# Gates of a mixture layer turned in 32x32 blocks by VectorE instead of 128x128 by TensorE, with one gate factor moved to ScalarE and GpSimd

## The chip, the cores and the metric

One core of a Trainium2 chip runs the whole program. Its five engines are named as in the profile: PE (TensorE, matrix products), DVE (VectorE), ACT (ScalarE), POOL (GpSimd) and SP (which only issues transfers here). The metric is the device time of one execution in microseconds (us), the median of several runs; lower is better.

## The reference, cut to what matters

Attention with mixed heads gives x, of 1792 tokens by 768. Two layers follow; the change lies in the first and in the part of the second that uses its gates. N is 1792, D 768, F 2048, and there are 32 slots (8 experts by 4).

```python
h = x @ w_in                          # 1792 x 2048
g = h - np.tanh(h)
x = g @ w_out                         # 1792 x 768
logits = x @ phi                      # 1792 x 32
d = softmax(logits, axis=0)           # over tokens
slot_input = d.T @ x                  # 32 x 768
slot_out[e] = relu(slot_input[e] @ w1[e]) @ w2[e]    # 8 experts
c = softmax(logits, axis=1)           # over slots
out = c @ slot_out
```

The product `g @ w_out` is never formed. The kernel folds w_out and phi into `wphi` (2048 x 32), so that logits = g @ wphi; it keeps `SA`, the sum over tokens of d times g (32 x 2048), and multiplies that with w_out at the end.

## The kernel before, in words

**Stages.** Up to about 496 us the attention runs; the first two products of the next stage already stand between its last matmuls. `moe_and_slots` then works through the tokens in four passes of 512, 512, 512 and 256 tokens (`PASS`). A pass has 16 steps, one for each 128 columns of w_in; step t = 16 b + f is step f of pass b. After the last step come the logits of the last pass, the slot sums, the products with w_out, and the eight experts (`hidden`, `finish`, `slot_out`, from 840 us), whose weights stream in through a ring of buffers of 1536 KB (`free`, `give`, `load_expert`).

**A step.** `step(t)` issues everything by hand: each engine runs its instructions in the order in which the code gives them. `product(t)` is 18 matmuls (6 blocks of 128 inputs, three terms each: high and low parts of weight and input) into one of three PSUM banks. Between the six blocks it calls the hooks that `on(c, ...)` has put there. While PE forms product t, the other engines work on the gate of step t-1: `gate_act` (ACT: square of h into `sq`, a second square with a shift into `qd`, tanh into `g`, a mask `mk`), `gate_poly` and `gate_first` (DVE: two products that finish the polynomial in `qd`, then h - tanh), and `gate_last` (DVE: the third product, then the polynomial is copied where h is small). `sq` lies in the PSUM banks q0 and q1.

**The turn.** The slot sums contract over tokens, but a gate has the 128 columns on partitions and tokens along the row. So `turn_g(t-2)` lets PE transpose the gate in 128x128 blocks into PSUM (four matmuls in the first three passes, two in the last; tile `gt`), and ACT copies the result into one of five `quad` buffers (L826, L829). In the next pass `slot_turn` does the same for the exponentials of the 32 slots (`etp`, L946), and `slot_sum`, in two halves in steps 4 and 5, multiplies: 4 token blocks by 4 groups of columns, each a matmul with 128 rows, 32 columns of weights and 512 columns of data into one of the four 32-partition strips of one bank (L958). One DVE instruction adds the bank to `SA` (L966). After the last step the same is done for the last pass, and `dt` (L1152) turns `SA` with four matmuls.

**Weights.** In the first pass ACT and POOL split each weight tile into high and low parts (`split_w`, L707 and L708) and store both for the next passes (`wis`); the first pass also turns w_out (`wt`). In the last pass the tile is loaded anew and split in halves: `split_half(t+1, 0)` on DVE and `split_half(t+1, 1)` on ACT, with the low parts from POOL (L717).

Of the kernel before, what the change touches and what calls it, by code (L numbers as in the profile page):

```python
# [566 lines left out]
def moe_and_slots(tc, ident, xd, wi, wo, wo4, wis, consts, w1, w2, out, box):  # L567
# [5 lines left out]
    tshift, tlimit, phi, sel, sela, seld = consts  # L573
# [17 lines left out]
    XW = KD * TM  # L591
    RU = 2 * DM
# [29 lines left out]
    quad, quad_a, quad_b = [xep.tile([128, FB * NRM], FP32, tag=f"quad{i}", name="quad") for i in range(3)]  # L622
# [120 lines left out]
    hps, quads, tok = {}, {}, {}  # L743
# [26 lines left out]
    def gate_act(t, beside=None):  # L770
        hp = hps[t]
        if t > 1:
            mem["sq"] = {t: bank(f"q{t % 2}", [128, PASS[t // NF]], "sq")}
        sq, qd, mk, g = temps_of(t)
        nc.scalar.activation(out=sq, in_=hp, func=ACTF.Square)  # L775
        nc.scalar.activation(out=qd, in_=sq, func=ACTF.Square, bias=tshift)
        if t >= LAST:
            gate_poly(t)
# [39 lines left out]
    def turn_g(t):  # L818
        b, f = divmod(t, NF)
        n = blocks[b]  # L820
        if f % NG == 0:
            tok[b, f // NG] = place(b, f // NG)
        g = g_of(t)
# [3 lines left out]
        i = f % NG  # L827
        dst = tok[b, f // NG].rearrange("p (r f) -> p r f", r=n)[:, :, i * 128:(i + 1) * 128]
        nc.scalar.activation(out=dst, in_=x, func=ACTF.Copy)  # L829

    def place(b, k):
        if b == NPASS - 1:
            n = blocks[b] * FB
            return quads["C" if k < 2 else "D"][:, k % 2 * n:(k % 2 + 1) * n]
        return quads["AECDB"[(b * NQ + k) % 5]]
# [571 lines left out]
```

## Time and profile before

| | |
|---|---|
| median of 3 runs | 930.33 us (929.08 to 930.88) |
| the profiled execution | 929.89 us |
| its span, first to last instruction | 928.2 us |
| mean granted TensorE clock | 0.988 of full speed |
| busy, share of the span | PE 97%, PEld 71%, DVE 61%, ACT 62%, POOL 32% |

The profile is one execution. PE is TensorE's matmuls and PEld its weight loads, which run beside them. A matmul of plain 32-bit floats shows as two records, one of the fp32r kind as one, a transpose as one. A row with a tile name `a<-b` writes a and reads b. Idle time is put down to what ended it.

### The profile page before, as it was taken

The page shows a single profiled execution, that of the slowest core. Times are in us where ns is not written, and L with a number is a line of the kernel's source. Part 1 is how long each engine was busy: PE and PEld are TensorE (multiplying, and loading weights), DVE is VectorE, ACT ScalarE, POOL GpSimd, SP SyncE. Part 2 cuts the span into 40 slices and gives each one's busy share as a digit, 9 for nine tenths or more (in the row PEclk, how much of TensorE's full clock was granted, in tenths as well). Part 3 has the DMA queues.
Part 4 walks back from the last instruction along what each step waited for, and adds up shares of the span by engine and source line. Part 5 has one row for each costly group of instructions (what it writes and reads, how often), then busy time and mean ns, then how long its engine had stood idle before and what let it go on. Part 6 is the DMA issues. An engine that isn't in the chain of part 4 may idle for free.

```text
span 928.2 us, 19426 instructions
## 1 busy us (share of the span) xinstructions
PE 898.9 (97%) x6926; PEld 659.8 (71%) x6926; DVE 564.2 (61%) x1267; ACT 574.0 (62%) x1299; POOL 296.5 (32%) x499
## 2 busy tenths in 40 slices
PE   8999999999999999999999999999999999999995
PEld 6667777777777777777777777767776776874542
DVE  3576667767577676786555567567766776740104
ACT  4776767777677777777666576646664665730113
POOL 1464445644456444565432222000000014610000
PEclk9999999999999999999999999999999999998997
DMA  6988688976889567674467868769764445879997
GB/s 134 241 219 234 190 242 226 235 216 200 230 233 267 179 201 215 205 249 145 144 238 246 324 232 269 257 243 365 290 226 157 155 131 187 314 297 425 422 389 279
DMA packets 143988, 223.95 MB, mean 241 GB/s; under 512 B 60756, under 2 KB 125332, under 8 KB 140052
## 3 DMA queue, kind: packets, MB, share of 16 engines
q1 hardware_dynamic: 140544, 209.83, 70.3%
q10 hardware_dynamic: 3348, 12.87, 3.6%
q8 instruction: 56, 0.92, 0.4%
q14 instruction: 40, 0.33, 0.1%
HBM read 147.96 MB, written 36.18 MB: 198 GB/s over the span
## 4 chain that ended last, share of the span: by engine, by line
PE 90%; DMA 3%; ACT 3%; DVE 2%; issue 1%; POOL 0%; ACTq 0%; POOLq 0%; SPq 0%; DVEq 0%
PE hp L755 24%; PE pm L297 15%; PE tm L333 14%; PE vx L357 8%; PE sc L266 7%; PE h L1195 3%; DMA D<-S 3%; PE gt L826 3%; PE so L1234 2%; PE tz L1213 2%; PE lgp L876 2%; PE sp L958 1%; PE wt L845 1%; PE qx L245 1%; PE wp L857 1%
## 5 line engine op out<-in xcount | busy, mean ns | idle before, releaser
L333 PEld LDWEIGHTS tm<-wk,e 120*112 120x112 f32 (+1 forms) x1440 | 174.0, 177 | 70.7 <-issue 58.9
L299 DVE TENSOR_REDUCE mx<-pm 120x1 f32<-120x448 f32 x180 | 111.9, 622 | 125.2 <-PE pm L297 124.6
L336 ACT ACTIVATE aT<-tm 112x480 f32<-112x480 f32 x180 | 105.4, 586 | 120.5 <-PE tm L333 120.5
L297 PE MATMUL pm<-D,wpre 120*120 120x448 f32 x360 | 174.2, 566 | 3.8 <-DMA D<-S 2.2
L333 PE MATMUL tm<-wk,e 120*112 120x120 f32 (+1 forms) x1440 | 176.7, 266 | 1.0 <-POOL wk L323 1.0
L323 POOL TENSOR_SCALAR wk<-wpost,rv 120x120 f32<-120x120 f32 x180 | 125.0, 695 | 136.2 <-PE tm L333 115.2
L755 PE MATMUL hp<-xa,rg 128*128 128x512 f32 x576 | 152.5, 405 | 0.0
L755 PEld LDWEIGHTS hp<-xa,rg 128*128 128x128 f32 x576 | 102.4, 188 | 28.5 <-issue 10.7
L306 ACT ACTIVATE e<-pm,mx 120x448 f32<-120x448 f32 x180 | 113.5, 631 | 4.9 <-DVE rv L318 2.3
L717 POOL TENSOR_TENSOR rg<-rg 128x384 fp32r<-128x384 f32 x32 | 32.0, 1013 | 207.9 <-DVE rg L714 193.8
L274 ACT ACTIVATE S<-sc 120x448 f32<-120x448 f32 (+1 forms) x186 | 90.7, 543 | 5.3 <-PE sc L266 3.0
L357 PE MATMUL vx<-aT,vn 112*64 112x120 f32 (+1 forms) x1536 | 84.0, 262 | 0.0
L786 DVE SCALAR_TENSOR_TENSOR qd<-qd,sq 128x512 f32<-128x512 f32 (+1 forms) x62 | 38.3, 617 | 71.6 <-ACT mk L782 63.5
L357 PEld LDWEIGHTS vx<-aT,vn 112*64 112x64 f32 x1536 | 73.9, 137 | 6.2 <-issue 1.1
L775 ACT ACTIVATE sq<-hp 128x512 f32<-128x512 f32 (+1 forms) x62 | 32.9, 530 | 72.6 <-PE hp L755 72.6
L755 PE MATMUL hp<-xb,rg 128*128 128x512 f32 x288 | 74.7, 404 | 0.0
L312 POOL TENSOR_SCALAR rv<-ss 120x1 f32<-120x1 f32 x180 | 43.0, 239 | 96.8 <-ACT e L306 84.6
L297 PEld LDWEIGHTS pm<-D,wpre 120*120 120x120 f32 x360 | 51.4, 182 | 26.4 <-issue 11.4
L266 PE MATMUL sc<-khi,qT 64*120 64x448 f32 (+1 forms) x384 | 68.8, 387 | 0.8 <-DVE qT L249 0.8
L68 POOL TENSOR_TENSOR fa<-fa,f 128x384 f32<-128x384 f32 x64 | 65.3, 1020 | 5.3 <-issue 0.3
L755 PEld LDWEIGHTS hp<-xb,rg 128*128 128x128 f32 x288 | 52.0, 188 | 16.6 <-issue 6.3
L708 POOL TENSOR_TENSOR rg<-rg 128x768 fp32r<-128x768 f32 x13 | 24.0, 1844 | 67.9 <-PE gt L826 33.5
(173 smaller groups left out, 1356.9 us busy)
## 6 DMA issues: line engine op xcount, KB each, us to landing
ex<-in_moe_w_dram SPq DMA_DIRECT2D x25, 1536.0 KB
D<-S SPq DMA_DIRECT2D x172, 210.0 KB
rg<-wis SPq DMA_DIRECT2D x32, 768.0 KB
f<-in_moe_w_in_dram SPq DMA_DIRECT2D x32, 384.0 KB
f<-in_moe_w_out_dram SPq DMA_DIRECT2D x32, 384.0 KB
wis<-rg ACTq DMA_DIRECT2D x16, 768.0 KB
rg<-wi SPq DMA_DIRECT2D x26, 384.0 KB
wi<-fa SPq DMA_DIRECT2D x32, 192.0 KB
```

Source lines behind the costliest of these rows:

```text
L68: eng.tensor_tensor(out=out, in0=bits(a), in1=bits(p), op=ALU.add)
L266: nc.tensor.matmul(xs[e][0][:ni], lhsT=qT[n][s, l, p, :ni], rhs=kt[s], start=(i == 0), stop=(i == 2))
L274: nc.scalar.activation(out=dst, in_=xs[e][0][:ni], func=ACTF.Copy)
L297: nc.tensor.matmul(x[:r], lhsT=wpre[:r, :m, :], rhs=D_t.pop(s)[:r], start=True, stop=True)
L299: nc.vector.tensor_reduce(out=mx[:r], in_=x[:r], op=ALU.max, axis=AX.X, negate=True)
L306: nc.scalar.activation(out=e[:r], in_=pp_t.pop(s)[:r], func=ACTF.Exp, bias=mx_t.pop(s)[:r], accum_out=ss[:r])
L312: nc.gpsimd.tensor_scalar(out=rv[:r], in0=ss_t.pop(s)[:r], scalar1=EPS, scalar2=None, op0=ALU.add)
L323: nc.gpsimd.tensor_scalar(out=wk[:r], in0=wpost[:r], scalar1=ss_t.pop(s)[:r], scalar2=None, op0=ALU.mult)
L333: nc.tensor.matmul(x[:, c, :, :m], lhsT=e[:r, c * JP:(c + 1) * JP], rhs=wk[:r, :, :m], start=True, stop=True)
L336: nc.scalar.activation(out=attn_t[n][:, :, :, c0:c0 + m], in_=x[:, :, :, :m], func=ACTF.Copy)
L357: nc.tensor.matmul(x[64 * e:64 * e + 64, i, :ni], lhsT=nat_v[b, h // NP][:, h % NP, c, :], rhs=a[:, c, h, :ni], start=(c == 0), stop=(c == ...
L755: nc.tensor.matmul(hp, lhsT=r32(w[:, m, hl, cs]), rhs=r32(x_of(b, c, l)), start=(c == 0 and i == 0), stop=(c == KD - 1 and i == 2))
```

## The change

It turns the gates on DVE. `turn_g` becomes one or two DVE transposes that turn every 32x32 block of a gate in place of PE's 128x128 transposes and ACT's copy; the blocks go to `turned[0]` (`tq`) and `turned[1]` (`th`), 8 token blocks of 32 each. They hold one pass, so the turns of steps 0 to 2 of a pass wait until its step 4, behind the slot sum of the pass before (in the first pass those of steps 0 to 4 wait until step 6). `slot_turn` is one DVE transpose. `slot_sum` is a single piece at the end of step 3: 64 matmuls of 32 rows by 32 columns with 512 columns of data (32 in the last pass), in four banks (q0, q1, r0, r1) by four strips. `SA` grows to 128 x 2048 and takes four DVE updates; `dt` takes 16 matmuls.

The gate: `sq` moves to SBUF, ACT forms `sa` = sq - A, POOL multiplies it with sq, and DVE's two products of the polynomial become one (steps 2 to 47). In the last pass both split copies go to ACT, behind the two squares. Three `quad` buffers become one of twice the size; the last pass gives two buffers instead of three to the experts' ring. The scratch for dynamic transfers goes from 1024 to 256 bytes.

```diff
     def split_half(t, m):
             h, l = unit(t)[:, m, 0], unit(t)[:, m, 1]
-            if m == 0:
-                nc.vector.tensor_copy(out=r32(h), in_=l)
-            else:
-                nc.scalar.activation(out=r32(h), in_=l, func=ACTF.Copy)
+            nc.scalar.activation(out=r32(h), in_=l, func=ACTF.Copy)
             nc.gpsimd.tensor_tensor(out=r32(l), in0=l, in1=h, op=ALU.subtract)
...
     def gate_act(t, beside=None):
-            mem["sq"] = {t: bank(f"q{t % 2}", [128, PASS[t // NF]], "sq")}
+            mem["sq"] = {t: mem["sb"][:, :PASS[t // NF]]}
         nc.scalar.activation(out=sq, in_=hp, func=ACTF.Square)
+        if 1 < t < LAST:
+            sa = mem["sa"][:, :PASS[t // NF]]
+            nc.scalar.activation(out=sa, in_=sq, func=ACTF.Identity, bias=tminus)
+            nc.gpsimd.tensor_tensor(out=sa, in0=sa, in1=sq, op=ALU.mult)
         nc.scalar.activation(out=qd, in_=sq, func=ACTF.Square, bias=tshift)
...
     def gate_first(t):
-        if t < LAST:
-            gate_poly(t)
+        if 1 < t < LAST:
+            nc.vector.scalar_tensor_tensor(out=qd, in0=qd, scalar=TG_E, in1=sa, op0=ALU.add, op1=ALU.mult)
         nc.vector.tensor_tensor(out=g, in0=hp, in1=g, op=ALU.subtract)
...
     def turn_g(t):
         b, f = divmod(t, NF)
-        x = turn_bank([128, n, 128], "gt")
-        for r in range(n):
-            nc.tensor.transpose(out=x[:, r, :], in_=g[:, r * 128:(r + 1) * 128], identity=ident)
-        nc.scalar.activation(out=dst, in_=x, func=ACTF.Copy)
+        g = g_of(t).rearrange("p (b l) -> p b l", l=NSL)
+        for part in range(0, PASS[b] // NSL, NTB // 2):
+            nc.vector.transpose(out=turned[part * 2 // NTB][:, :, f, :], in_=g[:, part:part + NTB // 2, :])
...
-    def slot_sum(b, lo, hi):
+    def slot_sum(b):
+        n = PASS[b] // NSL
+        xs = [bank(tag, [128, NF, NSL], "sp") for tag in ("q0", "q1", "r0", "r1")]
+        for tb in range(n):
+            g = tb % NG
+            rows = turned[tb * 2 // NTB][:, tb % (NTB // 2)]
+            for i in range(NG):
+                p = slice(NSL * i, NSL * i + NSL)
                 nc.tensor.matmul(
-                    x[NSL * k:NSL * k + NSL, :], lhsT=es[:, r, :], rhs=tok[b, k][:, r * FB:(r + 1) * FB],
+                    xs[i][NSL * g:NSL * g + NSL], lhsT=es[p, tb * NSL:(tb + 1) * NSL], rhs=rows[p],
+                    start=(tb < NG), stop=(tb >= n - NG))
+        for i in range(NG):
+                nc.vector.scalar_tensor_tensor(out=s, in0=s, scalar=a, in1=xs[i], op0=ALU.mult, op1=ALU.add)
...
-    dt = bank("h2", [128, NG, 128], "dt")
-    for i in range(NG):
+    dt = bank("h2", [128, NF, NSL], "dt")
+    for i in range(NF):
         nc.tensor.matmul(dt[:, i, :], lhsT=mem["SA"][:, i * 128:(i + 1) * 128], rhs=sr, start=True, stop=True)
...
-    nc = _bacc.Bacc("TRN2", target_bir_lowering=False, num_devices=1, dynamic_dma_scratch_size=1024)
+    nc = _bacc.Bacc("TRN2", target_bir_lowering=False, num_devices=1, dynamic_dma_scratch_size=256)
```

**What moves on PE, second pass, steps 3 and 4.** Of the kernel before (`hp` is a step's product, `gt` a turn of a gate, `etp` that of the exponentials, `sp` the slot sum of the first pass):

```order
L826 MATMUL gt<-ident,g 128x128 x4
L755 MATMUL hp<-xb,rg 128x512 x6
L946 MATMUL etp<-ident,et 128x32 x4
L755 MATMUL hp<-xb,rg 128x512 x12
L826 MATMUL gt<-ident,g 128x128 x4
L755 MATMUL hp<-xb,rg 128x512 x3
L958 MATMUL sp<-quad,es 32x512 x2
L958 MATMUL sp<-tq,es 32x512 x2
```

and of the change, from the small products of step 2 on:

```order
L882 MATMUL ln<-seld,lp 128x32 x4
L754 MATMUL hp<-xb,rg 128x512 x27
L946 MATMUL sp<-tq,es 32x512 x32
L946 MATMUL sp<-th,es 32x512 x32
L754 MATMUL hp<-xb,rg 128x512 x36
L865 MATMUL lgp<-g,wphi 32x512 x4
```

The turns are gone, the slot sum stands in one piece behind step 3, and its matmuls are 64 where they were 16.

**What moves on DVE, one step late in the third pass (`xc` is the next pass's tokens being split).** Before:

```order
L786 SCALAR_TENSOR_TENSOR qd<-qd,sq 128x512
L787 SCALAR_TENSOR_TENSOR qd<-sq,qd 128x512
L794 TENSOR_TENSOR g<-hp,g 128x512
L799 SCALAR_TENSOR_TENSOR hp<-qd,hp 128x512
L800 COPY_PREDICATED g<-mk,hp 128x512
L741 TENSOR_TENSOR xc<-xc 128x256
```

and now (`L797` is the shortened polynomial, `STREAM_TRANSPOSE` the turn):

```order
L797 SCALAR_TENSOR_TENSOR qd<-qd,sa 128x512
L798 TENSOR_TENSOR g<-hp,g 128x512
L803 SCALAR_TENSOR_TENSOR hp<-qd,hp 128x512
L804 COPY_PREDICATED g<-mk,hp 128x512
L824 STREAM_TRANSPOSE tq<-g 128x8x32
L824 STREAM_TRANSPOSE th<-g 128x8x32
L740 TENSOR_TENSOR xc<-xc 128x256
```

One product of the polynomial goes, two turns of 256 columns each come.

**What moves on ACT, one step of the last pass.** Before:

```order
L775 ACTIVATE sq<-hp 128x256
L776 ACTIVATE qd<-sq,tshift 128x256
L716 ACTIVATE rg<-rg 128x384
L781 ACTIVATE g<-hp 128x256
L782 ACTIVATE mk<-sq,tlimit 128x256
L829 ACTIVATE tq<-gt 128x2x128
```

and now:

```order
L774 ACTIVATE sq<-hp 128x256
L779 ACTIVATE qd<-sq,tshift 128x256
L715 ACTIVATE rg<-rg 128x384 x2
L784 ACTIVATE g<-hp 128x256
L785 ACTIVATE mk<-sq,tlimit 128x256
```

The copy of a turned gate (`L829`) goes, and the first split copy, DVE's before, comes in behind the second square.

## Rows read from the trace of the kernel before

**Rows 1.** The page, parts 1 and 4: engines' busy time; the chain by engine

```profile
PE 898.9 (97%) x6926; PEld 659.8 (71%) x6926; DVE 564.2 (61%) x1267; ACT 574.0 (62%) x1299; POOL 296.5 (32%) x499
...
PE 90%; DMA 3%; ACT 3%; DVE 2%; issue 1%; POOL 0%; ACTq 0%; POOLq 0%; SPq 0%; DVEq 0%
```

**Rows 2.** Windows: stretch, length, busy us per engine (instructions), PE clock, DMA share, GB/s

```profile
501.00:585.50 84.50, 82.59 (x460) 61.02 (x459) 54.20 (x89) 57.14 (x101) 22.12 (x12) 1.00 0.79 274
...
760.00:818.00 58.00, 52.64 (x408) 43.63 (x408) 41.56 (x110) 38.91 (x102) 29.96 (x30) 0.97 0.65 225
...
840.00:905.00 65.00, 62.96 (x687) 30.76 (x686) 4.92 (x19) 7.03 (x14) 2.17 (x8) 0.92 1.02 411
```

**Rows 3.** Timeline of PE, two steps of the third pass: start us, length us

```profile
733.22 4.36 PE L755 MATMUL hp<-xa,rg 128*128 128x512 f32 x18
...
737.77 4.35 PE L755 MATMUL hp<-xa,rg 128*128 128x512 f32 x18
```

**Rows 4.** The chain: start, length, what ran; one half of a slot sum, one step's product

```profile
614.27 1.92 PE sp L958 x16
...
738.01 4.11 PE hp L755 x18
```

**Rows 5.** The chain, in the last pass: a wait for a weight load

```profile
801.63 7.04 DMA rg<-wi
```

**Rows 6.** Timeline of SP's queue: loads issued after the last product, first and last group

```profile
817.85 4.53 SPq L673 DMA_DIRECT2D ex<-in_moe_w_dram  x3
...
870.11 26.96 SPq L673 DMA_DIRECT2D ex<-in_moe_w_dram  x3
```

**Rows 7.** Lines by form, 640 to 660 us (after the bar: busy us, mean ns)

```profile
L782 ACT ACTIVATE mk<-sq,tlimit 128x512 f32<-128x512 f32 x4 | 2.8, 690 | 0.0
...
L787 DVE SCALAR_TENSOR_TENSOR qd<-sq,qd 128x512 f32<-128x512 f32 x4 | 2.8, 691 | 0.1
```

**Rows 8.** Lines by form, 790 to 799 us, in the last pass

```profile
L717 POOL TENSOR_TENSOR rg<-rg 128x384 fp32r<-128x384 f32 x7 | 7.0, 1018 | 2.9 <-PE hp L755 2.6 <-DVE qd L786 0.4
...
L794 DVE TENSOR_TENSOR g<-hp,g 128x256 f32<-128x256 f32 x4 | 1.7, 413 | 0.0
```

**Rows 9.** Lines by form, 526 to 563 us, in the first pass

```profile
L708 POOL TENSOR_TENSOR rg<-rg 128x768 fp32r<-128x768 f32 x6 | 11.1, 1845 | 27.8 <-PE gt L826 18.7 <-ACT rg L707 9.1
...
L707 ACT ACTIVATE rg<-rg 128x768 fp32r<-128x768 f32 x6 | 5.0, 834 | 0.0
...
L787 DVE SCALAR_TENSOR_TENSOR qd<-sq,qd 128x512 f32<-128x512 f32 x5 | 3.5, 691 | 0.2
```

**Rows 10.** Lines: the update of the slot sums

```profile
L966 DVE SCALAR_TENSOR_TENSOR SA<-SA,al,sp 128x512 f32<-128x512 f32 x3 | 2.2, 748 | 3.0 <-PE sp L958 3.0
```

**Rows 11.** Timeline of ACT in the last pass

```profile
796.45 0.39 ACT L775 ACTIVATE sq<-hp 128x256 f32<-128x256 f32 x1
796.87 0.47 ACT L776 ACTIVATE qd<-sq,tshift 128x256 f32<-128x256 f32 x1
797.30 0.52 ACT L716 ACTIVATE rg<-rg 128x384 fp32r<-128x384 f32 x1
```

**Rows 12.** Timeline of PE, starts of the slot sum's records in the second pass

```profile
614.27 0.62 PE L958 MATMUL sp<-quad,es 128*32 128x512 f32 x2 [0.41 <-ACT quad L829]
614.28 0.62 PE L958 MATMUL sp<-tq,es 128*32 128x512 f32 x2
614.72 0.60 PE L958 MATMUL sp<-quad,es 128*32 128x512 f32 x2
```

**Rows 13.** The chain, one group of scores in the attention stage

```profile
296.14 1.41 PE sc L266 x12
```

**Rows 14.** Timeline of PE, 32 small matmul records of the attention stage

```profile
289.79 1.43 PE L357 MATMUL vx<-aT,vn 112*64 112x88 f32 x32
```

**Rows 15.** Timeline of PE: small outputs in pass two; the stage before the experts

```profile
603.00 0.97 PE L893 MATMUL ln<-seld,lp 128*128 128x32 f32 x8
...
828.73 1.16 PE L1152 MATMUL dt<-sr,SA 128*128 128x128 f32 x8 [0.59 <-DVE sr L1149]
```

More of the change, by code (lines that the diff above doesn't have):

```diff
@@ L621, in moe_and_slots @@
     xbuf = {0: [xap.tile([128, XW], FP32, tag=f"x{l}", name="xa") for l in range(2)]}
-    quad, quad_a, quad_b = [xep.tile([128, FB * NRM], FP32, tag=f"quad{i}", name="quad") for i in range(3)]
+    turned = [None, xep.tile([128, NTB // 2, NF, NSL], FP32, tag="th", name="th")]
+    quad = turned[1].rearrange("p b f l -> p (b f l)")
     ring = [w.rearrange("p (m h i) -> p m h i", m=2, h=2) for w in (rg[:, :RU], rg[:, RU:], *rgs)]
@@ L942, in slot_turn @@
         a, et = es_in[b]
-        n = blocks[b]
-        xe = turn_bank([128, n, NSL], "etp")
-        for r in range(n):
-            nc.tensor.transpose(out=xe[:, r, :], in_=et[:NSL, r * 128:(r + 1) * 128], identity=ident[:NSL, :NSL])
-        es = keep.tile([128, NRM, NSL], FP32, tag="es", name="es")
-        nc.scalar.activation(out=es[:, :n], in_=xe, func=ACTF.Copy)
+        es = (mem["tz"] if b == NPASS - 1 else keep).tile(
+            [128, PASS[b]], FP32, tag="es" if b == NPASS - 1 else "lp", name="es")
+        nc.vector.transpose(out=es, in_=et)
         es_in[b] = (a, es)
-    def slot_sum(b, lo, hi):
+    def slot_sum(b):
         a, es = es_in[b]
-        if lo == 0:
-            mem["sum"] = bank("r1", [128, FB], "sp")
-        x = mem["sum"]
-        for r in range(lo, hi):
-            for k in range(NQ):
-                nc.tensor.matmul(
-                    x[NSL * k:NSL * k + NSL, :], lhsT=es[:, r, :], rhs=tok[b, k][:, r * FB:(r + 1) * FB],
-                    start=(r == 0), stop=(r == blocks[b] - 1))
-        if hi < blocks[b]:
-            return
-        mem["sum"] = None
-        s = mem["SA"][:, :FB]
-        if b:
-            nc.vector.scalar_tensor_tensor(out=s, in0=s, scalar=a, in1=x, op0=ALU.mult, op1=ALU.add)
-        else:
-            nc.vector.tensor_copy(out=s, in_=x)
+        n = PASS[b] // NSL
[5 more added lines that the diff above has]
+                p = slice(NSL * i, NSL * i + NSL)
+                nc.tensor.matmul(
+                    xs[i][NSL * g:NSL * g + NSL], lhsT=es[p, tb * NSL:(tb + 1) * NSL], rhs=rows[p],
+                    start=(tb < NG), stop=(tb >= n - NG))
+        sums = mem["SA"].rearrange("p (f i l) -> p i f l", i=NG, l=NSL)
+        for i in range(NG):
+            s = sums[:, i]
+            if b:
+                nc.vector.scalar_tensor_tensor(out=s, in0=s, scalar=a, in1=xs[i], op0=ALU.mult, op1=ALU.add)
+            else:
+                nc.vector.tensor_copy(out=s, in_=xs[i])
     pieces, folds = {}, {5: 0, 9: 1, 13: 2, 16: 3}
@@ L1001, in step @@
             on(1, gate_first, t - 1)
-        on(4 if t > LAST + 2 else 2, turn_g, u)
         if ws:
@@ L1015, in step @@
         if b and f == 3:
-            on(4, slot_turn, b - 1)
+            on(1, slot_turn, b - 1)
             on(KD, gates_last, b - 1)
-        if b and f in (4, 5):
-            on(3, slot_sum, b - 1, 2 * f - 8, 2 * f - 6)
+            on(KD, slot_sum, b - 1)
         if t > 2:
             on(4, gate_last, t - 1)
+        if b == 0 and f < 7:
+            if f == 6:
+                for i in (1, 0, 2, 3, 4):
+                    on(4, turn_g, i)
+        elif f < 2 or f > 4:
+            on(4, turn_g, u)
+        elif f == 4:
+            for i in range(3):
+                on(4, turn_g, t - 4 + i)
         if b + 1 < NPASS:
@@ L1046, in step @@
                 zp = whole.enter_context(tc.tile_pool(name="m_z", bufs=1, reuse_waits="tile"))
-                for i in range(3):
+                for i in range(2):
                     give(zp.tile([128, EXB], FP32, tag=f"z{i}", name="ex"))
```

53 lines of the change are left out of this document (23 added, 30 removed).

## The prediction

> **What bounds the kernel now.** I begin with the page. PE is busy for 97% of the span and holds 90% of the chain of waits; DVE, ACT and POOL have 61, 62 and 32% [rows 1]. So work taken off PE counts at once, if the engines that get it stay hidden, and this has to be asked stage by stage. The windows answer [rows 2]: in the first pass PE is busy 82.59 of 84.50 us at a granted clock of 1.00; in the last pass 52.64 of 58.00, so there other engines and loads hold it up; from 840 us PE is nearly full again, with the DMA engines at 1.02 and 411 GB/s. The timeline of PE gives a step late in the third pass: 737.77 − 733.22 = 4.55 us from product to product [rows 3]. The chain gives the product alone, 4.11 us, and half a slot sum, 16 records (8 matmuls) in 1.92 us [rows 4]. In the last pass the chain stands for 7.04 us on a weight load [rows 5]. Behind the last product SP issues the remaining loads of expert weights, 23 in all, from 817.85 to 870.11 us [rows 6]: the experts run beside the transfers.
>
> **A. Turns off PE, steps 2 to 47.** A step becomes 4.55 − 4.11 = 0.44 us shorter [rows 3, 4], if nothing else is slower. 46 × 0.44 = **−20.2 us**. The cover: DVE has four gate products of about 0.69 us [rows 7] and two turns. No row shows a DVE transpose. The nearest is an instruction with 256 columns, 0.413 us [rows 8]; at half that rate it were 0.83. I take 0.42, since a turn reads one operand where that row reads two. DVE then needs 4 × 0.69 + 2 × 0.42 = 3.6 us of 4.11. ACT has five instructions over 512 columns (four before), at 0.69 each [rows 7] 3.5 us, and POOL a product of 512 columns, between 1.02 us for 384 and 1.85 for 768 [rows 8, 9]: about 1.29. All hidden. Step 4 of a pass is full: three updates of the slot sums more, 0.75 each [rows 10], and three gates' turns at once: 2.8 + 4 × 0.75 + 6 × 0.42 = 8.3 us, so DVE falls 4.2 us behind and regains 0.5 per step. A product needs its PSUM bank only three steps after that bank's last product, so almost two steps of lag (8 us, less the 3.5 us that a gate's own work takes) are covered: just enough.
>
> A first rule of the Trainium skill speaks against giving POOL this work. The row first: DVE's product takes 691 ns in the first pass, where POOL is busy 22.12 of 84.5 us [rows 2, 9], and 691 ns in the stretch behind it [rows 7]. The page "GPSIMD Engine Reference", in its section of key points, says that GpSimd shares its way to SBUF with VectorE and that the two contend. The trace shows no such loss at this load; by the rule DVE's 3.6 us would grow, and the rival on DVE below gain weight.
>
> **B. First pass.** POOL also makes the low parts of the next weight tile. Its product of the gate needs ACT's first two instructions; then 0.69 × 3 for ACT's squares and the new factor, 0.83 for the high parts, 1.85 for the low parts [rows 7, 9] stand in series: 4.75 us. Steps there are about 84.50/16 = 5.28 us with what else they hold, 4.84 without the turn. That is tight, so I allow **+1 us**, bounds 0 and +4.
>
> **C. Last pass.** Of the 58.0 us [rows 2], waits on turns, the turns and waits on loads go: a first turn is not on PE, and one buffer fewer goes to the experts' loads that compete with them. What is left is a cycle per step: ACT's two squares and the first split copy, 797.30 + 0.52 − 796.45 = 1.37 us [rows 11], POOL's low parts 1.02 [rows 8], and about 0.2 for the handoffs: 2.6 us. 16 × 2.6 = 41.6, one slot sum 3.7 [rows 4], and about 3.6 us at the start, where DVE still has a 512-column gate: 49 us. DVE however has five gate products and one turn of 256 columns, 6 × 0.42 = 2.5 us of the 2.6, and carries 4 × 0.75 + 2 × 0.42 = 3.8 us more at the slot sum, which it can hardly regain: I add 2. 51 − 58 = **−7 us**, bounds −9.5 and −3.
>
> **D. The slot sum.** Three run inside the loop, and half of one (256 tokens) behind it: 3.5 sums. Before, 16 matmuls of 128 rows take 2 × 1.85 = 3.7 us [rows 4], four at a time in four column strips [rows 12]: each runs 4 × 3.7/16 = 0.93 us, in two records of about 0.45. Now 64 of 32 rows have as many columns of data each. Sixteen at a time they take 64 × 0.93/16 = 3.7 us, the same: **0**. Four column strips at a time are shown: four matmuls start within some 0.02 us and second records 0.45 behind [rows 12]. Row strips are shown for two: the scores, 12 records in 1.41 us, 0.117 each for 448 columns, where one alone would need about 0.2 (448 columns at the product's 4.11/18 for 512) [rows 4, 13]. How fast small records can start: 32 in 1.43 us, 0.045 each [rows 14]; 128 records at that rate need 5.7 us, so the bounds are 0 and 3.5 × 2 = +7.
>
> **E. Behind the loop.** Three more updates of the slot sums, 3 × 0.75 = +2.2 [rows 10]. The last turn of the slot sums takes 32 records instead of 8: at 0.97/8 = 0.12 [rows 15] 3.9 us against 1.16 [rows 15], +2.7. PE's path loses two turns of half the size, 2 × 0.22 (half of A's 0.44), and a wait for ACT's copy like the 0.41 ahead of the slot sum [rows 12], −0.9. **+4 us**, bounds +1 and +5. The experts' loads: 24 instead of 23 follow the last product, 1.57 MB at 411 GB/s [rows 2] = +3.8 us; PE also comes 4 us later to them, so no new wait.
>
> The scratch of 256 bytes I cost at nothing: the chain gives the issuing queues (SPq, POOLq, ACTq) 0% [rows 1]. Should it make them wait, the loads of the experts would show it, by the same 3.8 us per lost load.
>
> **Sum.** −20.2 + 1 − 7 + 0 + 4 = −22.2. The profiled execution took 929.89 us, so 907.7; the median of the runs stands 0.44 above it: **908.1 us**. A measurement here tells about 0.2%, 1.9 us, from no change.
>
> **Rivals.**
> 1. *Slot sum eight at a time* (the second record of a matmul holds back the row strips beside it). For: no row shows four row strips at once, only two [rows 13]. Against: column strips lose nothing [rows 12]. 64 × 0.93/8 = 7.4, +3.7 × 3.5 = +13: 921 us. Chance 0.13.
> 2. *Four at a time, the kernel slower.* If row strips of one column don't run side by side in this order (the code takes the four row strips of one column strip one behind the other), a sum takes 64 × 0.93/4 = 14.8 us, +11.1 × 3.5 = +39: 947 us. It decides as follows: the rest gains 22.2, 6.3 per sum, so a sum over 10 us, fewer than 6 at a time, makes the kernel slower. For: the two-strip row is not a full halving [rows 13]. Chance 0.11.
> 3. *Strictly in order*: the second record of a matmul waits for its first, and nothing issued behind it starts meanwhile. 64 × 0.45 = 28.8 us per sum, +25 × 3.5 = +88: 996 us. Against: four matmuls start together, their second records all later [rows 12]. Chance 0.02. Beside it stands a rule: the Trainium skill, "TensorE: Matmul & The Clock Gate", Part 3 (the mechanism), says that matmuls start and end in program order, with no reordering. The same part measures 10.6-fold speed for sixteen 32x32 tiles, which would put a sum near 5.6 us by estimate. The trace agrees with tiles running together, for column strips; no run here shows sixteen tiles.
> 4. *DVE becomes the bound*: a turn takes 0.83 us. Then a step needs 4 × 0.69 + 1.66 = 4.4, the gain of A falls to 46 × 0.13 = 6, and the last pass comes to 5 × 0.42 + 0.83 = 2.95 per step, some 55 us. −6 + 1 − 3 + 4 = −4: 926 us. It decides from a turn of 0.67 us on. For: the instruction is in no row. Chance 0.07.
> 5. *Other engines give part back*: the first pass slips at POOL (+4), the step-4 backlog of DVE stalls a product or two (+2), the last pass runs at 2.8 us (+3): 917 us. Chance 0.09.
> That the change doesn't do what it says is excluded by the order of the instructions: no turn is left on PE.
>
> **How the numbers follow.** The forecast has 0.56; the rivals 0.13, 0.11, 0.02, 0.07, 0.09; 0.02 is left for what I don't see. The forecast's own range, from the bounds: −20.2 − 9.5 + 1 and a little more on the low side (900), to the +7 of D or so (917). To leave out no more than 2 in 10 the range must take in rival 1 and 5: 900 to 924, with rivals 2 to 4 outside (0.20). Faster: forecast, 1, 4 and 5 without a little, 0.83. Slower: rivals 2 and 3 and a rest, 0.14. Within 0.2%: 0.03.
>
> **What would show it.** Right: steps of 4.1 us in the second and third pass with no gaps; a slot sum of 3.7 to 5.7 us; a DVE turn near 0.4 us; a last pass near 51 us from its first product to its last; POOL products near 1.3 us, four slot-sum updates of 0.75 in a row, and `dt` near 4 us. Wrong: a slot sum of 7.4 or 14.8 us (rivals 1, 2); steps of 4.4 with PE waiting for DVE (4); gaps ahead of products that end with POOL's low parts in the first pass (5); new waits on expert weights past 840 us, which would mean that the freed time was bounded by the transfers.

## The result and the profile after

The changed kernel takes 935.67 us (median of 20 runs, 928.70 to 938.51), the kernel before on the same chips 929.00 (median of 20). One execution of the kernel before, at 1266.09 us, stands apart from the other 19 (926.50 to 932.24) and is left out of the ratio. The ratio is 1.0063, 95% interval [1.0048, 1.0078]: **slower by 0.6%**, where 908.1 us, 2.4% faster, was forecast. The profiled execution has a span of 931.7 us against 928.2. The page and the chain of waits of the changed kernel, as in [rows 1]:

```profile
PE 886.4 (95%) x7048; PEld 648.5 (70%) x7048; DVE 597.4 (64%) x1333; ACT 582.4 (63%) x1293; POOL 365.1 (39%) x546
...
PE 77%; DVE 12%; DMA 4%; ACT 3%; issue 2%; POOL 1%; ACTq 0%; DVEq 0%; SPq 0%; POOLq 0%
```

PE has 12.5 us less work, as it should, but its share of the chain falls from 90 to 77%, and DVE's rises from 2 to 12%. DVE, which was to be hidden, sets the pace in many places. Which, the stages tell. Each is measured in the timeline of PE, from the first product of a pass to that of the next:

| stage, us | before | after | difference | forecast |
|---|---|---|---|---|
| ahead of the first product | 482.7 | 481.3 | −1.4 | 0 |
| first pass (A, B) | 102.8 | 104.5 | +1.7 | −5.2 |
| second pass (A, D) | 89.6 | 83.1 | −6.5 | −7.0 |
| third pass (A, D) | 85.2 | 78.2 | −7.0 | −7.0 |
| last pass, to the start of its last matmul (C, D) | 57.2 | 63.1 | +5.9 | −7 |
| from there to the end (E) | 110.7 | 121.5 | +10.8 | +4 |

The first row holds attention, which the change does not touch; in twelve other executions it lies between 481.1 and 484.6. The forecast of the second and third pass came true; the first, the last and the stage behind the loop are 7, 13 and 7 us over theirs. The windows that answer to two of [rows 2] show the same from another side:

```profile
501.00:585.50 84.50, 79.29 (x404) 56.74 (x403) 60.39 (x101) 58.73 (x100) 42.87 (x25) 0.96 0.76 267
...
760.00:818.00 58.00, 47.50 (x437) 37.90 (x435) 48.25 (x111) 34.41 (x88) 27.27 (x25) 0.94 0.54 185
```

In the first, PE now has 79.29 us of work in the 84.50 and stands idle for 5 us instead of 2; POOL is busy for 42.87 us instead of 22.12. The second is the same stretch of time, though the passes have moved ahead by 13 us in it: it holds the rest of the last pass and 8 us behind the loop. PE is busy 47.50 of 58.00 us there, at a granted clock of 0.94 instead of 0.97. The chain has the steps in order of time (start, length, what ran):

```profile
689.94 4.46 PE sp L946 x121
...
703.81 16.55 PE hp L754 x72
...
766.66 7.03 PE sp L946 x127
...
783.05 1.10 DVE qd L790
...
823.65 7.04 PE dt L1148 x32
...
831.70 6.29 PE si L1159 x64
```

Four products in a row take 16.55 us, 4.1 each: a step without its turn, as forecast ([rows 3, 4]). The slot sum takes 4.46 us, between the 3.7 of sixteen at a time and the upper bound of 5.7. In the last pass the chain runs over DVE's product L790, once per step and 1.1 us each, and over a slot sum of 7.03 us; behind the loop over a turn of the sums (`dt`) of 7.04 us. What happened to the DVE products, lines by form tell (count, busy us, mean ns). First pass, 500 to 586 us:

```profile
L710 POOL TENSOR_TENSOR rg<-rg 128x768 fp32r<-128x768 f32 x12 | 25.3, 2112 | 1.5 <-ACT rg L709 1.0
...
L797 DVE SCALAR_TENSOR_TENSOR qd<-qd,sa 128x512 f32<-128x512 f32 x13 | 15.7, 1211 | 9.4 <-POOL sa L778 9.4
```

Second pass, 640 to 670 us, and last pass, 782 to 810 us:

```profile
L797 DVE SCALAR_TENSOR_TENSOR qd<-qd,sa 128x512 f32<-128x512 f32 x7 | 4.8, 684 | 2.8 <-POOL sa L778 2.8
...
L824 DVE STREAM_TRANSPOSE tq<-g 128x256 f32<-128x256 f32 x6 | 2.6, 431 | 0.0
```

```profile
L790 DVE SCALAR_TENSOR_TENSOR qd<-sq,qd 128x256 f32<-128x256 f32 x9 | 10.2, 1130 | 0.3
L789 DVE SCALAR_TENSOR_TENSOR qd<-qd,sq 128x256 f32<-128x256 f32 x10 | 3.8, 383 | 0.0
```

L797, the shortened polynomial, needs 684 ns in the second pass and 1211 in the first. L790, a product of 256 columns, needs 1130 ns, while its neighbour L789 with the same operands needs 383. A turn into `tq` is 431 ns, one into `th` 404, as taken. The timeline shows what goes with the long ones (start, length; one step of the last pass):

```profile
785.62 0.38 DVE L789 SCALAR_TENSOR_TENSOR qd<-qd,sq 128x256 f32<-128x256 f32 x1
785.69 2.35 POOL L716 TENSOR_TENSOR rg<-rg 128x384 fp32r<-128x384 f32 x2 [0.66 <-ACT rg L715]
...
786.04 1.11 DVE L790 SCALAR_TENSOR_TENSOR qd<-sq,qd 128x256 f32<-128x256 f32 x1
```

POOL's two low-part products begin at 785.69 and need 1.17 us each, so the first ends at about 786.86. L789 began ahead of them and takes 0.38. L790 begins at 786.04, inside POOL's instruction, and ends at 787.15, some 0.3 us after POOL's first one. Its inputs `sq` and `qd` both lie in SBUF. In the kernel before, `sq` lay in PSUM, and from step 2 on no product of the gate read SBUF twice. This is the theory that the experiments test first: a DVE product with both inputs in SBUF and a POOL product hold each other up.

The other steps bear it out. Of the last pass's sixteen L790 twelve begin inside a POOL product, and all twelve end 0.27 to 0.29 us behind it; the other four take 0.42 to 0.43 us. Of the first pass's fourteen L797 six begin inside a POOL product; they end 0.54 to 0.55 us behind it and take 1.22 to 2.33 us, the other eight 0.68 to 0.69. Where DVE starts first, POOL pays, with 2.37 to 2.39 us for low parts that took 1.85 before ([rows 9]):

```profile
503.06 0.69 DVE L797 SCALAR_TENSOR_TENSOR qd<-qd,sa 128x512 f32<-128x512 f32 x1 [1.12 <-POOL sa L778]
503.08 2.39 POOL L710 TENSOR_TENSOR rg<-rg 128x768 fp32r<-128x768 f32 x1
```

What PE waited for (us in all, times, longest):

```profile
PE sp L946 <- DVE es L934: 7.7, 4, 4.5
PE hp L754 <- POOL rg L716: 5.2, 9, 0.9
PE lgp L865 <- DVE wphi L856: 4.7, 3, 2.7
PE dt L1148 <- DVE sr L1145: 2.4, 1, 2.4
```

The 4.7 us for `wphi` fall in the first pass: PE's logits wait there for DVE, which is late with the copies of the folded weights. For POOL's low parts PE waits 0.3 us in that pass.

And PE's granted clock (fourth number behind the window: length, PE busy, clock, DMA share, GB/s), in the two places where the chain had 7 us:

```profile
766.60:769.50 2.90, 2.84 (x52) 0.50 0.01 5
...
820.30:823.60 3.30, 0.91 (x9) 0.98 0.99 410
823.60:830.60 7.00, 6.95 (x33) 0.50 0.51 213
830.60:834.00 3.40, 3.40 (x25) 0.55 0.00 0
```

The last pass's sum begins after 4.5 us of waiting for the turned exponentials and runs at a granted clock of 0.50 (1.2 of 2.4 GHz) at first. Behind the loop PE waits 2.4 us for DVE's four updates and the factor `sr`; then `dt` runs at 0.50 throughout, and the products behind it begin at 0.55. The DMA engines fall to 0.51 and then to 0.00 there, where the kernel before has them at 0.99 or more.

### The profile page after: what moved, and what is told of

The parts are those of the page before. It is cut to its first block, busy times and chain, and to the rows that moved or that the text cites. A ratio compares the mean times of both kernels' runs of the same rounds, so it can differ in the third digit from the quotient of the medians.

```text
span 931.7 us, 19906 instructions
## 1 busy us (share of the span) xinstructions
PE 886.4 (95%) x7048; PEld 648.5 (70%) x7048; DVE 597.4 (64%) x1333; ACT 582.4 (63%) x1293; POOL 365.1 (39%) x546
## 4 chain that ended last, share of the span: by engine, by line
PE 77%; DVE 12%; DMA 4%; ACT 3%; issue 2%; POOL 1%; ACTq 0%; DVEq 0%; SPq 0%; POOLq 0%
PE hp L754 16%; PE pm L297 16%; PE tm L333 15%; PE vx L357 8%; PE sc L266 7%; PE h L1191 2%; DMA ex<-in_moe_w_dram 2%; PE sp L946 2%; PE so L1230 2%; DVE qd L797 1%; DVE qd L790 1%; PE tz L1209 1%; DVE g L804 1%; DMA D<-S 1%; DVE g L798 1%
## 5 line engine op out<-in xcount | busy, mean ns | idle before, releaser
L754 PE MATMUL hp<-xa,rg 128*128 128x512 f32 x576 | 146.6, 403 | 0.4 <-POOL rg L710 0.3
L754 PEld LDWEIGHTS hp<-xa,rg 128*128 128x128 f32 x576 | 105.6, 190 | 32.3 <-issue 10.7
L778 POOL TENSOR_TENSOR sa<-sa,sq 128x512 f32<-128x512 f32 x46 | 60.6, 1318 | 160.4 <-ACT sa L777 160.4
L754 PE MATMUL hp<-xb,rg 128*128 128x512 f32 x288 | 70.5, 400 | 0.0
L297 PEld LDWEIGHTS pm<-D,wpre 120*120 120x120 f32 x360 | 51.4, 182 | 25.3 <-ACT e L306 10.6
L754 PEld LDWEIGHTS hp<-xb,rg 128*128 128x128 f32 x288 | 53.3, 188 | 17.6 <-issue 5.5
L797 DVE SCALAR_TENSOR_TENSOR qd<-qd,sa 128x512 f32<-128x512 f32 x46 | 40.0, 869 | 32.9 <-POOL sa L778 32.9
L754 PE MATMUL hp<-xc,rg 128*128 128x256 f32 x288 | 40.7, 292 | 6.0 <-POOL rg L716 5.2
```

The source lines that it names most:

```text
L297: nc.tensor.matmul(x[:r], lhsT=wpre[:r, :m, :], rhs=D_t.pop(s)[:r], start=True, stop=True)
L754: nc.tensor.matmul(hp, lhsT=r32(w[:, m, hl, cs]), rhs=r32(x_of(b, c, l)), start=(c == 0 and i == 0), stop=(c == KD - 1 and i == 2))
L778: nc.gpsimd.tensor_tensor(out=sa, in0=sa, in1=sq, op=ALU.mult)
```

## The experiments

Ratios are to the kernel before, on the same chip. Each stands against 1.0063 of the change.

**1. The square in PSUM, last pass only** (e1_square_in_psum).

```diff
-            mem["sq"] = {t: mem["sb"][:, :PASS[t // NF]]}
+            mem["sq"] = {t: bank(f"q{t % 2}", [128, PASS[-1]], "sq") if t >= LAST else mem["sb"][:, :TM]}
```

> The square of h lies in a PSUM bank again in the last pass; all else as in the changed kernel. Theory (two inputs from SBUF): a DVE instruction that reads both inputs from SBUF waits for POOL's low-part product, 1.12 us where it took 0.42. Then the second polynomial product falls from about 1.1 to 0.42 us, a step of the last pass from 3.0 to about 2.5, ten such steps give -5 us, and the whole comes to about 0.6% less than the changed kernel (ratio to before near 1.001). Rival (the slot sum and the loads set the last pass): the product gets short, but the steps stay at 3.0 us, and the ratio stays at 1.006.

Measured: 1.0022 [1.0001, 1.0044]. Nothing but the place of one operand was changed, and the product is short again (lines by form, 784 to 810 us):

```profile
L790 DVE SCALAR_TENSOR_TENSOR qd<-sq,qd 128x256 f32<-128x256 f32 x10 | 4.2, 425 | 0.3
```

The last pass falls from 63.1 to 58.3 us, by 4.8. The theory holds for this pass.

**2. The shifted square in PSUM, steps 2 to 47** (e2_shifted_in_psum).

```diff
-        nc.scalar.activation(out=qd, in_=sq, func=ACTF.Square, bias=tshift)
+        if 1 < t < LAST:
+            mem["qp"] = bank(f"q{t % 2}", [128, TM], "qd")
+        nc.scalar.activation(out=mem["qp"] if 1 < t < LAST else qd, in_=sq, func=ACTF.Square, bias=tshift)
...
-            nc.vector.scalar_tensor_tensor(out=qd, in0=qd, scalar=TG_E, in1=sa, op0=ALU.add, op1=ALU.mult)
+            nc.vector.scalar_tensor_tensor(out=qd, in0=mem["qp"], scalar=TG_E, in1=sa, op0=ALU.add, op1=ALU.mult)
```

> In steps 2 to 47 ACT writes the shifted square to a PSUM bank, so that DVE's one product of the polynomial reads one input from SBUF and one from PSUM. Theory (two inputs from SBUF): that product falls from a mean of 1.21 us in the first pass to 0.69, POOL's low parts from 2.2 to 1.85, and the first pass from 104.5 to about 99 us; ratio to before near 1.001. Rival (the chain through POOL is too long by itself, its product ahead of its low parts): DVE's product gets short, but the first pass stays within 1 us of 104.5, ratio 1.005 to 1.007.

Measured: 0.9957 [0.9941, 0.9973], faster than the kernel before. Lines by form of the first pass, 500 to 586 us:

```profile
L710 POOL TENSOR_TENSOR rg<-rg 128x768 fp32r<-128x768 f32 x12 | 22.6, 1882 | 0.5
...
L799 DVE SCALAR_TENSOR_TENSOR qd<-qd,sa 128x512 f32<-128x512 f32 x14 | 9.6, 686 | 11.4 <-POOL sa L778 11.4
```

Both engines gain: DVE's product 1211 to 686 ns, POOL's low parts 2112 to 1882. The first pass falls from 104.5 to 97.3 us, more than expected. PE's wait for DVE's `wphi` falls from 4.7 to 1.2 us: it was DVE's lateness that held PE up. The chain through POOL that the rival speaks of is there but fits.

**3. The slot sum a step later** (e3_sum_later).

```diff
-            on(KD, slot_sum, b - 1)
+        if b and f == 4:
+            on(KD, slot_sum, b - 1)
...
-        elif f < 2 or f > 4:
+        elif f < 2 or f > 5:
             on(4, turn_g, u)
-        elif f == 4:
-            for i in range(3):
-                on(4, turn_g, t - 4 + i)
+        elif f == 5:
+            for i in range(4):
+                on(4, turn_g, t - 5 + i)
```

> The slot sum stands at the end of step 4 instead of step 3, and the turns that wait for it at step 5. Theory (the sum comes before its exponentials are turned): PE's wait of 4.55 us ahead of the last pass's sum falls under 1 us, the sum there runs at the full clock (7.03 to 4.46 us), and the sums of the two other passes lose about 1 us of waiting each: -8 us, ratio near 0.998. Rival (DVE is behind): the wait only moves, since three updates more and four gates' turns now stand together on DVE; PE waits a step later for its bank, and the ratio stays within 0.002 of 1.006.

Measured: 1.0026 [1.0007, 1.0046]; half of what was expected. What PE waited for from 740 us on:

```profile
PE hp L754 <- DVE qd L789: 2.8, 1, 2.8
...
PE sp L946 <- DVE es L934: 0.6, 1, 0.6
```

The wait for the exponentials falls from 4.5 to 0.6 us and the sum to 4.95, but a step later a product waits 2.8 us for DVE, whose queue L790 still holds up. Theory and rival are each half right: the last pass falls by 1.2 us, the second and third by 1.1 and 1.6.

**4. PE kept busy ahead of `dt`** (e4_warm_longer): `warm(3)` behind the last sum becomes `warm(13)`.

> Behind the last slot sum PE does 13 idle products instead of 3, over the 2.4 us in which it waited for DVE. Theory (the granted clock fell in that wait): the last turn of the slot sums runs at a granted clock near 1.00 instead of 0.50 and takes about 3.9 us instead of 7.04; all that follows starts 3 us earlier, ratio near 1.003. Rival (the end is set by the experts' loads): the turn gets short, but the kernel by less than 1 us, ratio 1.005 to 1.006.

Measured: 1.0061 [1.0041, 1.0081], no gain. The chain behind the loop, and PE's clock there (as above):

```profile
827.03 4.16 PE dt L1148 x32
...
832.21 7.71 PE si L1159 x64
```

```profile
823.60:827.00 3.40, 3.23 (x34) 1.00 1.03 412
827.00:831.20 4.20, 4.17 (x33) 0.88 0.83 346
...
833.00:836.00 3.00, 3.00 (x25) 0.50 0.16 30
```

`dt` itself is short, 4.16 us, but the clock falls all the same, now towards its end, and the stage behind it (`si`) pays: 7.71 us instead of 6.29. PE was busy 3.23 of the 3.40 us ahead of `dt`, so the wait was not the whole cause; `dt` itself, 32 records of 32 columns, is what is left, and v2 below tries that. From the last product to the experts' first one the kernel does gain 1.4 us (30.3 instead of 31.7), and loses it there, for that product runs at a lower clock than in the changed kernel (the second line):

```profile
843.80:848.40 4.60, 4.50 (x25) 0.63 1.02 425
841.90:844.80 2.90, 2.79 (x25) 1.00 1.00 424
```

So the gain failed to come as the rival has it, but the granted clock took most of it. Whether the loads would have taken it otherwise stays open: PE waits 0.8 us for them here and 2.1 in the changed kernel, but in either chain it stands on one of them (30.19 and 18.44 us).

**5. The kernel before with the square in SBUF, last pass** (e5_before_square_in_sbuf): one tile `sb` more, and the scratch of 256 bytes to make its room.

```diff
-            mem["sq"] = {t: bank(f"q{t % 2}", [128, PASS[t // NF]], "sq")}
+            mem["sq"] = {t: mem["sb"] if t >= LAST else bank(f"q{t % 2}", [128, TM], "sq")}
```

> The kernel before, with one thing of the change: in the last pass the square of h lies in SBUF (and the scratch is 256 bytes, which makes the room). No turn, no sum and no split copy is moved. Theory (two inputs from SBUF): the second polynomial product, 0.42 us before, waits for POOL's low-part products of about 1.0 us wherever the two meet, and takes some 0.6 to 1.1 us on the mean; 13 steps by up to 0.5 us, so the last pass becomes 2 to 6 us longer, ratio 1.002 to 1.006. Rival (it takes the new order of the split copies too): the product stays near 0.42 us and the ratio within 0.001 of 1.

Measured: 1.0006 [0.9988, 1.0024]. Lines by form of this kernel, 770 to 817 us:

```profile
L787 DVE SCALAR_TENSOR_TENSOR qd<-sq,qd 128x256 f32<-128x256 f32 x14 | 13.7, 978 | 0.5
```

and of the kernel before, in the same stretch:

```profile
L787 DVE SCALAR_TENSOR_TENSOR qd<-sq,qd 128x256 f32<-128x256 f32 x14 | 5.9, 424 | 0.5
```

There this product takes 0.42 us, like its neighbours (0.413 in [rows 8]); now 0.98. The mechanism is shown without any other part of the change than the scratch, which experiment 8 tries alone. The time is not: the last pass grows by 1.4 us only (57.2 to 58.7), no more than it differs between the kernel before and experiment 8 (55.7), and the whole by nothing that can be measured. The expected loss was too high; that DVE had room there is likely and not shown.

**6. The factor back on DVE, square still in SBUF** (e6_factor_back_on_dve).

```diff
-        if 1 < t < LAST:
-            sa = mem["sa"][:, :PASS[t // NF]]
-            nc.scalar.activation(out=sa, in_=sq, func=ACTF.Identity, bias=tminus)
-            nc.gpsimd.tensor_tensor(out=sa, in0=sa, in1=sq, op=ALU.mult)
...
-            sa = mem["sa"][:, :PASS[t // NF]]
-            nc.vector.scalar_tensor_tensor(out=qd, in0=qd, scalar=TG_E, in1=sa, op0=ALU.add, op1=ALU.mult)
+            gate_poly(t)
```

> Of the changed kernel, ACT's factor and POOL's product are taken out; DVE makes both products of the polynomial in steps 2 to 47, from the square in SBUF. Theory (two inputs from SBUF): both products now read SBUF twice, and in the first pass they still meet POOL's low parts, so the first pass stays at 102 us or more; in the second and third pass DVE needs 5 x 0.69 + 2 x 0.42 = 4.3 us of a step of 4.1 to 4.2 and cannot regain what the slot sum costs it, +3 to +8 us over both; ratio 1.006 to 1.015. Rival (POOL's gate product is what costs the first pass): the first pass falls to 97 to 99 us, ratio under 1.004.

Measured: 1.0079 [1.0053, 1.0105]. Both products, 500 to 586 us, and PE's largest wait there:

```profile
L786 DVE SCALAR_TENSOR_TENSOR qd<-sq,qd 128x512 f32<-128x512 f32 x12 | 16.0, 1333 | 0.4
L785 DVE SCALAR_TENSOR_TENSOR qd<-qd,sq 128x512 f32<-128x512 f32 x12 | 11.7, 978 | 0.0
```

```profile
PE lgp L860 <- DVE wphi L851: 6.8, 3, 4.2
```

The first pass takes 106.8 us, as the theory has it: with POOL's gate product gone, its low parts alone hold both products up. But the second and third pass did not grow; they take 82.7 and 77.8 us, 0.4 less than with the factor on POOL. DVE's 4.3 us per step fit, because a step with its share of the logits is 4.4 on the mean (17.6 us for four in the third pass), not 4.1.

With the factor gone POOL does nothing at all in the second pass, and that gives a control that nobody planned. L740, the split of the next pass's tokens, was in the kernel before and has both inputs in SBUF. In the second pass of the changed kernel, beside POOL's factor, and then of this experiment:

```profile
L740 DVE TENSOR_TENSOR xa<-xa 128x512 fp32r<-128x512 f32 x6 | 6.2, 1027 | 0.0
L740 DVE TENSOR_TENSOR xa<-xa 128x512 fp32r<-128x512 f32 x6 | 3.9, 651 | 0.0
```

**7. The gate of the kernel before, all else changed** (e7_gate_of_before): as 6, and `sq` in the banks q0 and q1 throughout.

> The changed kernel with the gate of the kernel before: square in PSUM in all passes, both polynomial products on DVE, no factor on ACT and POOL. Turns, sum and split copies stay as changed. Theory (two inputs from SBUF are the loss, the factor moved to POOL gains nothing): first pass 96 to 99 us, second and third about 82.7 and 77.9 as with the factor back on DVE, last pass about 58.3 as with the square in PSUM; ratio 0.991 to 0.996. Rival (DVE needs the relief, with 5 x 0.69 + 2 x 0.42 = 4.3 us per step and the fold's copies in the first pass): the first pass stays over 101 us, ratio over 0.998.

Measured: 1.0037 [1.0014, 1.0059]; the expectation missed. The first pass takes 100.4 us, better than 104.5 but 3 more than in the second experiment, the second and third 83.7 and 81.2, the last 60.7. In the first pass the rival has a point: PE waits 2.7 us for DVE's `wphi`, against 1.2 in the second experiment. In the third pass DVE is busy 70.70 of 81.20 us, against 62.61 of 78.20 of the change, but that is not what costs there: experiment 6 has the same DVE work, 70.20 of 77.90 us, and loses nothing. In these two passes 6 and 7 differ by the place of the square alone, so the 1.0 and 3.4 us between them come from that place. The likely reason is that the square shares the banks q0 and q1 with the slot sum (in v4 below, with the same gate, the sum waits 1.3 us for DVE's product); no run separates it.

**8. The scratch alone** (e8_before_scratch_256).

> The kernel before with the scratch of 256 bytes alone. Theory (it costs nothing): ratio within 0.001 of 1. Rival (it holds transfers up): the loads of the experts come later and the ratio is over 1.002.

Measured: 0.9993 [0.9978, 1.0008]. It costs nothing.

**9. The order inside the slot sum** (e9_sum_by_row_strip): the loops over `tb` and `i` exchanged, nothing else.

> The changed kernel with the two loops of the slot sum exchanged: all token blocks of one row strip first, so that consecutive products share the row strip and come back to the same 32x32 tile after four. Theory (a product starts only after the one ahead of it in the program has started, so sixteen tiles run together only if sixteen different ones follow each other): four at a time, 4 x 3.7 = 14.8 us instead of 4.46, in the second and third pass; 10 us each, 5 behind the loop, and +10 or more in the last pass. Rival (the queue looks ahead, or the order does not matter): 4.5 us as before.

Measured in one execution: 972.38 us. The chain has the sum of the third pass as

```profile
708.76 14.66 PE sp L946 x128
```

14.66 us is what was expected, 64 x 0.93/4 = 14.9, but the number is luck. Its two parts are eight tiles at a time, for most of it, and half the clock. The timeline of PE at the start of this sum, and PE's granted clock from 711.90 us on (before that 1.00):

```profile
708.76 1.92 PE L946 MATMUL sp<-tq,es 32*32 32x512 f32 x16 [1.46 <-DVE es L934]
710.50 0.61 PE L946 MATMUL sp<-th,es 32*32 32x512 f32 x4
710.53 0.63 PE L946 MATMUL sp<-tq,es 32*32 32x512 f32 x4
...
711.36 0.61 PE L946 MATMUL sp<-th,es 32*32 32x512 f32 x4
```

```profile
711.90:723.40 11.50, 11.50 (x97) 0.50 0.00 0
```

A row strip has sixteen products, eight with data from `tq` and then eight from `th`. The first eight go four at a time. The other eight, from 710.50 on, run beside the first eight of the next row strip (`tq` again): eight at a time. Groups come every 0.43 us, and every 0.85 us once the clock has fallen; PE was busy all through the sum. Counted at the full clock, this sum is worth some 3.1 + 0.5 x 11.5 = 8.9 us (an estimate), 6.7 tiles at a time on the mean, against 4.46 us in the kernel's order. So the order does matter, by a factor of two, but the theory's account of it fails: the next row strip's first products start at 710.53, before the last four of the strip ahead at 711.36, which stand in front of them in the program. The exchange also lets sixteen products in a row write one bank, where the kernel's order goes round four; which of the two costs was not separated.

**10 to 12. Versions.** v1_three_edits takes the edits of 1, 2 and 3 together.

> The square of the last pass and the shifted square of steps 2 to 47 in PSUM banks, and the slot sum at the end of step 4 (the first three experiments together). If their gains add: ratios 1.0022, 0.9957 and 1.0026 against 1.0063 of the changed kernel give 1.0063 - 0.0041 - 0.0106 - 0.0037 = 0.988, 918 us. Rival (the sum put later gains only because DVE is late, and DVE is late only because of POOL): the third adds little to the first, ratio 0.990 to 0.992.

Measured: 0.9900 [0.9885, 0.9915], 918.98 us, which is the rival's sum rather than the 0.988 of gains that add. The three experiments leave that open, since each is known to some 0.002 only; that the third edit and the first remove partly the same wait is likely and not shown.

v2_two_stage_turn adds a new turn of the sums:

```diff
+    slot_sum(b)
+    warm(12)
+    dx = bank("h2", [128, FB], "dx")
+    for k in range(NQ):
+        nc.tensor.matmul(dx[NSL * k:NSL * k + NSL, :], lhsT=sr, rhs=mem["SA"][:, k * FB:(k + 1) * FB], start=True, stop=True)
+    warm(3)
+    ds = tq[:, :FB]
+    nc.scalar.activation(out=ds[:, :FB // 2], in_=dx[:, :FB // 2], func=ACTF.Copy)
+    nc.vector.tensor_copy(out=ds[:, FB // 2:], in_=dx[:, FB // 2:])
+    dt = bank("lg", [128, NG, 128], "dt")
+    for i in range(NG):
+        nc.tensor.transpose(out=dt[:, i, :], in_=ds[:, i * 128:(i + 1) * 128], identity=ident)
```

> As v1_three_edits, and the last turn of the slot sums in two stages: four products of 512 columns that run beside each other and add up the four token strips, a copy by ACT and DVE, four transposes of 128 columns; its factor is formed ahead of the sum, and PE does idle products in the wait. Theory (32 short products of 32 columns, at a granted clock that falls to 0.50 in them): they took 7.0 us, or 4.2 and then a slow stage behind them; now about 0.95 + 0.5 + 0.65 us, and the stage behind it at the full clock in 5.8 us: 4 to 6 us from the sum to the experts' first product, ratio 0.004 to 0.006 under v1. Rival (the experts' loads set the end): PE then waits for loads, and the ratio is within 0.002 of v1.

Measured: 0.9846 [0.9827, 0.9866], **915.56 us, the fastest version**, 2.2% under the changed kernel. PE behind the loop, and its clock in the stage that follows:

```profile
809.63 1.07 PE L1151 MATMUL dx<-SA,sr 128*32 128x512 f32 x8
...
811.40 0.70 PE L1158 MATMUL dt<-ident,tq 128*128 128x128 f32 x4
...
812.57 5.81 PE L1169 MATMUL si<-ex,wphi 128*32 128x384 f32 x64
```

```profile
812.00:815.00 3.00, 2.97 (x35) 1.00 0.73 311
```

The two parts take 1.07 and 0.70 us, and the clock stays at 1.00 in the stage that follows (`si`). From the loop's end to the experts' first product it is 25.1 us instead of 29.7 in v1. That product then takes 4.5 us at a granted clock of 0.62 instead of 2.8 at 1.00 in v1 (the kernel before has 4.5 at 0.63), so 1.7 of the 4.6 us are lost again. The ratio fell by 0.0054, as expected.

v4_gate_of_before is v2 with the gate of experiment 7.

> As v2_two_stage_turn, with the gate of the kernel before instead of the factor and the shifted square in PSUM. If the factor on ACT and POOL is worth nothing once no product reads SBUF twice: within 0.002 of the ratio 0.9846. If it relieves DVE where the sum and four gates' turns stand together: 0.002 to 0.006 above.

Measured: 0.9956 [0.9942, 0.9970], 0.011 above v2, more than either case had. So the factor on ACT and POOL, together with what it changes in the banks q0 and q1 (in v2 they hold the shifted square, in v4 the square), is worth about 10 us once no product of the gate reads SBUF twice; how much is due to either is not shown. As it was put in, it gained next to nothing (1.0063 with it, 1.0079 without it in experiment 6).

## Why the prediction was wrong

- **The rival on DVE, and the rule that was set aside.** The step that failed first is the sentence that the trace shows no loss when POOL works beside DVE. The row was true (691 ns in either pass) but answered another question: that product took one input from PSUM. The forecast took over the duration of a product and not the place of its operands, and the change moves `sq` to SBUF and adds `sa` there. The rule that the forecast set aside stands there without the condition that decides: the Trainium skill, "GPSIMD Engine Reference", section 8, has the contention for DVE instructions with two SBUF inputs; "SBUF — State Buffer", section "Who interferes with whom", says that whichever starts first keeps the shared ports for its whole instruction and the other blocks. The runs agree with both: L790 ends 0.3 us behind POOL's instruction, 1.13 us against 0.43 with one operand moved, and POOL's low parts grow from 1.85 to 2.39 us where DVE starts first.
- **A** was right for the second and third pass to 0.5 us, in part because two errors cancel: in the third pass the three steps around the slot sum gain 0.2 us instead of 1.3, the other thirteen 6.8 instead of 5.7. In the first pass 14 x 0.44 = 6.2 us were taken, and experiment 2 gives them back: 97.3 us, 5.5 under the kernel before, where −5.2 was forecast.
- **B**, +1 us with an upper bound of +4, was short: the loss is 7.2 us by experiment 2. Its chain of ACT and POOL was the wrong path: PE waited 0.3 us for POOL's low parts and 4.7 for DVE's `wphi`, since DVE's product and POOL's low parts both grew where they met. The 84.50/16 was misread as well: the window holds 13 steps, so a step there is 6.5 us on the mean (5.2 to 5.8 where nothing else stands in it) and the chain was less tight than it looked.
- **C**, −7, came out as +5.9. 4.8 us are L790 (experiment 1). Most of the other 8 are the slot sum: with L790 mended PE still waits 2.9 us for the turned exponentials, and the sum takes 6.0 us at a granted clock of 0.72, where 3.7 without a wait were forecast. That the change moves the sum ahead from steps 4 and 5 to the end of step 3, where its exponentials are not yet ready, has no term in the forecast: the added wait was missed. Moved back in v1, it returns 1.7 us. Even v2 needs 56.0 us where 51 were forecast: its steps come to 2.9 us instead of 2.6, and the chain still has a weight load (5.4 us); that the load's wait goes was wrong.
- **D**: 4.46 us instead of 3.7, within its bounds (the 1.85 of half a sum is not in [rows 4], which have 1.92; the price moves by 0.1). On the mean 13 of the sixteen tiles run together; rivals 1 to 3 fell, and with them the mechanism of the slower side. The rule of program order that stood beside the third rival (the Trainium skill, "TensorE: Matmul & The Clock Gate", Part 3) does not agree with experiment 9, where products start ahead of earlier ones of another row strip; the measurement decides. The 5.6 us estimated from that page's 10.6-fold speed were too high.
- **The other rivals**: a turn of 0.40 to 0.43 us ends the fourth. The fifth named the right places (the first pass, DVE behind the sum, the last pass), though its sign in the first pass, gaps that end with POOL's low parts, came to 0.3 us only; it priced them at 9 us together; 20 were lost in the first and last pass alone, and the time lies above the range.
- **E**, +4, came out as +10.8. `dt` at 0.12 us a record was 3.9 us; it took 4.16 us at a granted clock of 0.88 (experiment 4), but 7.04 at 0.50, and the clock has no term in the forecast. The updates of the sums were counted as work, +2.2, which is nearly what they cost (from the sum's end to `dt` 3.3 us instead of 1.4). The −0.9 for turns and a copy did not come: from PE's last matmul of the loop to the sum it is 7.8 us, before 7.9. "No new wait" on expert weights was wrong too: PE waits 2.1 us for them in the changed kernel and 3.0 in v2, and never in the kernel before. In v2 the stage is still 6 us longer than before.
- **The cover on DVE** (3.6 of 4.1 us a step) was not needed in the second and third pass: experiment 6 runs there with 4.3. It was in the first and last. Not every such product was cured: in v2 the split of the tokens still reads SBUF twice beside POOL, without a wait of PE in the second and third pass.

## What to carry to other kernels

Before work is moved to GpSimd, list for every VectorE instruction beside it where its two inputs lie: one operand moved to PSUM, a line or two of code, was worth 7.2 us in the first pass and 4.8 in the last. A duration holds for its operands' places as much as for its shape. When a step is put earlier, ask what its inputs wait for. Read the granted clock beside every duration of PE: 32 short matmuls cost twice here, by themselves and in the stage behind them, and in experiment 9 half the clock made a false account of the order come out at the right number.

## What was not expected of the hardware

- One DVE product of 256 columns took 1.13 us beside a POOL product and 0.43 with an input in PSUM; POOL lost too (2112 against 1882 ns for its low parts). The engine that started second ended 0.3 us (256 columns) or 0.5 us (512) behind the other.
- The granted clock fell to 0.50 behind 32 records of 32 columns, although PE had hardly been idle ahead of them (experiment 4); four products of 512 columns and four transposes in their place, with idle products ahead and between, left it at 1.00 there (v2). It then fell at the experts' first product, to 0.62, as in the kernel before (0.63).
- Sixteen 32x32 tiles gave 64 x 0.93/4.46 = 13 at a time. In another order of the same products eight ran together at most, and products of one row strip started ahead of earlier ones of another (experiment 9).
